# Moving two 8-byte state tiles behind the other pools of a fused scan and two-layer kernel

## The chip, the core and the metric

One core of a Trainium2 chip runs the whole program. The metric is the time of one execution in microseconds (us) as the device reports it; 2055.5 us is the median of three runs.

## The reference

For each of 4 sequences of 6080 steps with 256 features, a gated recurrence is computed, and its output goes through two matrix products with a squared ReLU between them:

```python
f = lower_bound + (1 - lower_bound) * sigmoid(f_logit)
for t in range(S):
    h = f[:, t] * h + (1 - f[:, t]) * x[:, t]
    y[:, t] = h
h = maximum(y.reshape(24320, 256) @ w_in, 0)     # w_in 256 x 2048
return h * h @ w_out                              # w_out 2048 x 256
```

Everything is float32. The kernel gets the precision on TensorE by splitting each operand into a high part (rounded to fp32r) and the rest (low part), and it takes three matmuls for one product: low weight with high data, high weight with high data, high weight with low data.

## The kernel before, in words

The 24,320 tokens lie along the free dimension, the 256 features on two blocks of 128 partitions. Tokens are taken in pairs of blocks of 512 (`pairs`, 23 pairs j = 0 to 22; the last pair, j = 23, has blocks of 384). For each pair, ScalarE, VectorE and GpSimd make the gate and the scan, and split the result into the tiles `xhi` and `xlo`, seven of each (`op_hi`, `op_lo`). Even pairs keep these in the pool `xA`, odd pairs in the pool `xB`.

The hidden layer has 16 blocks of 128 units, taken two at a time (q = 0 to 7). For the first two pairs (`plain`), each block is computed directly. From pair 2 on, `quad` computes two hidden blocks for two token blocks with seven products instead of eight (`product`, line 282, three matmuls each). The squared ReLU of the results is split again into `ghi` and `glo`, four pairs of tiles named `ghi00` to `ghi11` (`pair_of`, lines 316 and 317, in the pool `hid`). `layer2` (lines 303 to 305) multiplies them with the second layer's weights: six matmuls for each pair of tiles. In a quad the order on TensorE is written out: products P1, P5, P7; then `layer2` of the quad before for tile 00; P6, P2, P4, P3; then `layer2` for tiles 10, 01, 11. That is 21 matmuls with `xhi`/`xlo` as the moving operand ("x matmuls" below) and 24 with `ghi`/`glo` ("g matmuls"), 45 in a quad and 360 in a pair. Every matmul loads its own weights (PEld in the profile) while the matmul before it runs.

After a pair's last quad, `store` copies the sums on ScalarE into the one tile `osb` (line 312) and sends it out from SyncE's queue (line 313). It is called twice in the first quad of the next pair. The second call must wait until the first one's transfer has read the tile. In the quad behind it, ScalarE's copy at line 372 (`d`) is queued behind these copies, and P6 (the matmuls on `d`) needs it.

The order of instructions on each engine from the plain stage on is the program's own order (`manual_schedule`). The places of tiles in SBUF come from the pools: the pools of the left side follow each other in the order in which they are opened, and in a pool each tag follows the one before it, at the next multiple of 32 bytes. Starting bytes in a partition, as the program before has them:

| tiles | pool | start | start modulo 256 |
|---|---|---|---|
| weights `whi`, `wlo`, all 16, each column block of 128 | const | 16,608 and on, in steps of 512 | 224 |
| `xhi`, `xlo`, 14 tiles of 2048 bytes | xA | 106,720 and on | 224 |
| `f`, `x`, two buffers each of 4096 bytes | ld | 135,392 and on | 224 |
| `carry`, two buffers of 8 bytes | ld | 151,776 and 151,808 | 224, 0 |
| `ts` (sums for the products), two buffers | ld | 151,840 and on | 32 |
| `r`, `ghi`, `glo`, `s`, `c22`, `r22`, `c12` | hid | 155,936 and on (`ghi00` 160,032) | 32 |
| `osb`, 4096 bytes | outp | 188,704 to 192,800 | 32 |
| `xhi`, `xlo` of odd pairs (right side) | xB | 200,672 and on | 224 |

`carry` holds the last column of a pair's scan for the next pair; it is the only tile that isn't a multiple of 256 bytes long among the pools `xA`, `ld`, `hid` and `outp`.

Of the kernel before, what the change touches and what calls it, by code (L numbers as in the profile page):

```python
# [8 lines left out]
F32 = mybir.dt.float32  # L9
# [5 lines left out]
P = 128  # L15
# [17 lines left out]
def scan_then_relu2_kernel(  # L33
# [28 lines left out]
    KD = D // P  # L62
# [5 lines left out]
    ld = ctx.enter_context(tc.tile_pool(name="ld", bufs=1))  # L68
    hid = ctx.enter_context(tc.tile_pool(name="hid", bufs=1))
    outp = ctx.enter_context(tc.tile_pool(name="outp", bufs=1))  # L70
    ps = ctx.enter_context(tc.tile_pool(name="ps", bufs=1, space=bass.MemoryType.PSUM))

    xTv = xT.rearrange("(c p) t -> p c t", p=P)
# [16 lines left out]
    x_t, f_t, carry = {}, {}, {}  # L90
# [10 lines left out]
    def segments(t0, n):  # L101
        a = 0
        while a < n:
            s = (t0 + a) % seq
            m = min(n - a, seq - s)
            yield a, m, s == 0
            a += m
# [21 lines left out]
    def op_scan(j, t, c):  # L129
        t0, n = pairs[j]  # L130
        x = x_t[j, t]
        if t == 1 and c == 0:
            carry[j] = ld.tile([P, KD], F32, tag="carry", name=f"carry{j}", bufs=2)
        for a, m, new in segments(t0 + t * n, n):
            if new:
                init = 0.0
            elif a:
                init = x[:, c, a - 1 : a]
            elif t:
                init = x_t[j, 0][:, c, n - 1 : n]  # L140
            else:
                init = carry[j - 1][:, c : c + 1]
            nc.vector.tensor_tensor_scan(
                out=x[:, c, a : a + m], data0=f_t[j, t][:, c, a : a + m],
                data1=x[:, c, a : a + m], initial=init, op0=ALU.mult, op1=ALU.subtract,
            )
        if t == 1 and c == KD - 1 and j + 1 < NP:
            nc.vector.tensor_copy(carry[j][:, :], x[:, :, n - 1])
# [292 lines left out]
    def units(j):  # L441

        steps = []
        for t in range(2):
            for c in range(KD):
                steps.append([lambda t=t, c=c: op_sig(j, t, c), lambda t=t, c=c: op_f(j, t, c)])
                steps.append([lambda t=t, c=c: op_v(j, t, c)])
                steps.append([lambda t=t, c=c: op_scan(j, t, c)])

        def ready(*ks):  # L450
            out = []
            for k in ks:
                if k in MADE:
                    out.append(lambda k=k: op_sum(j, k, G))
                out += [lambda k=k: op_hi(j, k), lambda k=k: op_lo(j, k, G)]
            return out

        steps[6] += ready("B11")
        steps[7] += ready("B21")
        steps[9] += ready("T1")  # L460
        steps += [ready("T3"), ready("T2"), ready("T4"), ready("B22")]
        return steps

    def gate_ops(j, t, c, f_eng, lo_eng):
        k = f"B{c + 1}{t + 1}"
        return [
            lambda: op_sig(j, t, c),
            lambda: op_f(j, t, c, f_eng),
            lambda: op_v(j, t, c),
            lambda: op_scan(j, t, c),  # L470
            lambda: op_hi(j, k),
            lambda: op_lo(j, k, lo_eng),
        ]
# [52 lines left out]
    with tc.manual_schedule():  # L526
# [56 lines left out]
        j, q = before  # L583
# [45 lines left out]
```

## Time and profile before

| | |
|---|---|
| median of 3 runs | 2055.5 us (2054.15 to 2055.97) |
| the profiled execution's own time | 2055.8 us |
| its span, first to last instruction | 2054.0 us |
| TensorE (PE) busy, matmuls | 2002.1 us (97%), 8688 matmuls |
| weight loads (PEld) busy | 1627.1 us (79%) |
| VectorE (DVE) busy | 1536.5 us (75%) |
| ScalarE (ACT) busy | 1185.6 us (58%) |
| GpSimd (POOL) busy | 832.6 us (41%) |

A matmul's duration in the profile has a modelled end and overlaps with the next one's; the time from one matmul's start to the next one's start ("spacing" below) is what a matmul costs in an unbroken stream. Views of the trace print starts with two decimals of a microsecond, so a spacing over many matmuls is read from the first and the last start of the stretch.

### The profile page before, as it was taken

The page shows a single profiled execution, that of the slowest core. Times are in us where ns is not written, and L with a number is a line of the kernel's source. Part 1 is how long each engine was busy: PE and PEld are TensorE (multiplying, and loading weights), DVE is VectorE, ACT ScalarE, POOL GpSimd, SP SyncE. Part 2 cuts the span into 40 slices and gives each one's busy share as a digit, 9 for nine tenths or more (in the row PEclk, how much of TensorE's full clock was granted, in tenths as well). Part 3 has the DMA queues.
Part 4 walks back from the last instruction along what each step waited for, and adds up shares of the span by engine and source line. Part 5 has one row for each costly group of instructions (what it writes and reads, how often), then busy time and mean ns, then how long its engine had stood idle before and what let it go on. Part 6 is the DMA issues. An engine that isn't in the chain of part 4 may idle for free.

```text
span 2054.0 us, 24632 instructions
## 1 busy us (share of the span) xinstructions
PE 2002.1 (97%) x8688; PEld 1627.1 (79%) x8688; DVE 1536.5 (75%) x2283; ACT 1185.6 (58%) x2127; POOL 832.6 (41%) x712
## 2 busy tenths in 40 slices
PE   5999999999999999999999999999999999999998
PEld 3777787787878877878788787788887877878888
DVE  8975677777777777877778777777787777867765
ACT  4765555556555555555655555556555565555554
POOL 5747243443433424335344343443433424335332
PEclk9999999999999999999999999999999999999999
DMA  4211010101101011010110100101101011010000
GB/s 163 84 62 41 32 32 31 52 11 62 36 27 52 31 42 52 11 62 25 38 52 11 62 32 31 52 12 61 41 22 52 31 41 52 11 59 24 21 21 16
DMA packets 42013, 84.69 MB, mean 41 GB/s; under 512 B 2848, under 2 KB 4384, under 8 KB 41888
## 3 DMA queue, kind: packets, MB, share of 16 engines
q1 hardware_dynamic: 41888, 83.11, 12.1%
q8 instruction: 68, 1.11, 0.2%
q14 instruction: 57, 0.47, 0.1%
HBM read 58.20 MB, written 24.90 MB: 40 GB/s over the span
## 4 chain that ended last, share of the span: by engine, by line
PE 81%; DVE 6%; ACT 6%; DMA 4%; issue 2%; POOL 1%; SPq 0%; ACTq 0%; DVEq 0%; POOLq 0%
PE acc L303 14%; PE acc L305 14%; PE acc L304 14%; PE a L282 10%; PE c L282 10%; PE b L282 10%; PE d L282 6%; DMA out_dram<-osb 3%; ACT osb L312 2%; PE d L335 1%; DVE a L402 1%; DVE c L353 1%; ACT ghi L417 1%; DVE wy L223 1%; DVE c L392 1%
## 5 line engine op out<-in xcount | busy, mean ns | idle before, releaser
L303 PE MATMUL acc<-ghi,wlo 128*128 128x512 f32 (+1 forms) x1536 | 603.7, 393 | 6.1 <-ACT ghi L339 4.9
L305 PE MATMUL acc<-glo,whi 128*128 128x512 f32 (+1 forms) x1536 | 601.3, 391 | 3.3 <-DVE glo L343 3.1
L304 PE MATMUL acc<-ghi,whi 128*128 128x512 f32 (+1 forms) x1536 | 595.6, 388 | 0.0
L405 POOL TENSOR_TENSOR r<-r 128x512 f32<-128x512 f32 (+1 forms) x176 | 181.7, 1032 | 821.4 <-ACT ghi L403 622.7
L305 PEld LDWEIGHTS acc<-glo,whi 128*128 128x128 f32 x1536 | 288.8, 188 | 73.5 <-DVE glo L343 8.2
L303 PEld LDWEIGHTS acc<-ghi,wlo 128*128 128x128 f32 x1536 | 289.0, 188 | 66.0 <-ACT ghi L339 3.6
L304 PEld LDWEIGHTS acc<-ghi,whi 128*128 128x128 f32 x1536 | 288.9, 188 | 62.2
L356 ACT ACTIVATE ghi<-c 128x512 fp32r<-128x512 f32 (+1 forms) x176 | 110.6, 628 | 269.3 <-DVE c L353 269.3
L406 POOL TENSOR_TENSOR glo<-r,ghi 128x512 fp32r<-128x512 f32 (+1 forms) x176 | 226.7, 1288 | 13.8
L372 ACT ACTIVATE d<-a 128x512 f32<-128x512 f32 (+1 forms) x176 | 102.0, 579 | 210.1 <-PE a L282 209.6
L378 DVE TENSOR_TENSOR s<-b,s 128x512 f32<-128x512 f32 (+1 forms) x88 | 60.4, 686 | 215.4 <-ACT s L376 163.9
L182 POOL TENSOR_TENSOR xlo<-T,xhi 128x512 fp32r<-128x512 f32 (+1 forms) x88 | 114.2, 1297 | 137.8 <-ACT xhi L177 137.8
L358 DVE TENSOR_TENSOR glo<-c,ghi 128x512 fp32r<-128x512 f32 (+1 forms) x176 | 156.7, 890 | 2.8 <-ACT ghi L356 0.7
L378 DVE TENSOR_TENSOR s<-c,s 128x512 f32<-128x512 f32 (+1 forms) x88 | 60.3, 686 | 129.5 <-PE c L282 127.5
L182 POOL TENSOR_TENSOR xlo<-x,xhi 128x512 fp32r<-128x512 f32 (+1 forms) x72 | 93.0, 1293 | 146.5 <-ACT xhi L177 145.9
L282 PE MATMUL b<-xhi,wlo 128*128 128x512 f32 (+1 forms) x352 | 138.6, 394 | 0.3 <-DVE glo L419 0.3
L397 ACT ACTIVATE r<-a 128x512 f32<-128x512 f32 (+1 forms) x176 | 103.6, 589 | 61.1 <-PE a L282 61.1
L282 PE MATMUL a<-xhi,wlo 128*128 128x512 f32 (+1 forms) x352 | 138.8, 394 | 0.0
L282 PE MATMUL c<-xhi,wlo 128*128 128x512 f32 (+1 forms) x352 | 138.4, 393 | 0.0
L282 PE MATMUL a<-xlo,whi 128*128 128x512 f32 (+1 forms) x352 | 138.1, 392 | 0.0
L392 DVE TENSOR_TENSOR c<-d,s 128x512 f32<-128x512 f32 (+1 forms) x176 | 119.1, 677 | 24.8 <-PE d L282 20.5
L282 PE MATMUL b<-xlo,whi 128*128 128x512 f32 (+1 forms) x352 | 137.4, 390 | 0.0
(120 smaller groups left out, 4147.5 us busy)
## 6 DMA issues: line engine op xcount, KB each, us to landing
f<-in_fT_dram SPq DMA_DIRECT2D x46, 512.0 KB, 4.5
x<-in_xT_dram SPq DMA_DIRECT2D x46, 512.0 KB, 3.7
out_dram<-osb SPq DMA_DIRECT2D x46, 512.0 KB, 2.8
wraw<-in_wpack_dram SPq DMA_DIRECT2D x15, 512.0 KB, 3.3
f<-in_fT_dram SPq DMA_DIRECT2D x2, 384.0 KB, 3.5
x<-in_xT_dram SPq DMA_DIRECT2D x2, 384.0 KB, 3.2
out_dram<-osb SPq DMA_DIRECT2D x2, 384.0 KB, 2.4
wraw<-in_wpack_dram SPq DMA_DIRECT2D x2, 256.0 KB, 5.6
```

The source lines that it names most:

```text
L182: eng.tensor_tensor(out=xlo[j, i][:, :n], in0=block(j, k), in1=xhi[j, i][:, :n].bitcast(F32), op=ALU.subtract,)
L282: nc.tensor.matmul(bank[:, :n], lhsT=w, rhs=x[j, r][:, :n], start=start and m == 0, stop=m == 2, skip_group_check=True,)
L303: nc.tensor.matmul(acc, lhsT=lo, rhs=ghi[:, :n], start=first, stop=False)
L304: nc.tensor.matmul(acc, lhsT=hi, rhs=ghi[:, :n], start=False, stop=False)
L305: nc.tensor.matmul(acc, lhsT=hi, rhs=glo[:, :n], start=False, stop=last)
L356: nc.scalar.activation(out=ghi[:, :n], in_=c, func=AF.Copy)
L358: nc.vector.tensor_tensor(out=glo[:, :n], in0=c, in1=ghi[:, :n].bitcast(F32), op=ALU.subtract)
L378: nc.vector.tensor_tensor(out=sv, in0=bv, in1=sv, op=ALU.add)
L392: nc.vector.tensor_tensor(out=c22v, in0=dv, in1=sv, op=ALU.add)
L397: nc.scalar.activation(out=r11, in_=av, func=AF.Relu)
L405: nc.gpsimd.tensor_tensor(out=r22, in0=r22, in1=r22, op=ALU.mult)
L406: nc.gpsimd.tensor_tensor(out=lo22, in0=r22, in1=hi22.bitcast(F32), op=ALU.subtract)
```

## The change

A new pool `small` is opened after the pool `outp`, and the two buffers of `carry` are allocated there instead of in `ld`. Number of buffers, shapes, and all instructions with their order stay as they are.

```diff
     outp = ctx.enter_context(tc.tile_pool(name="outp", bufs=1))
+    small = ctx.enter_context(tc.tile_pool(name="small", bufs=1))
...
         if t == 1 and c == 0:
-            carry[j] = ld.tile([P, KD], F32, tag="carry", name=f"carry{j}", bufs=2)
+            carry[j] = small.tile([P, KD], F32, tag="carry", name=f"carry{j}", bufs=2)
```

The two places of 32 bytes go away from between `x` and `ts`. So `ts`, all of `hid` and `osb` start 64 bytes lower: `ts` at 151,776, `ghi00` at 159,968, `osb` at 188,640, and all of these starts are 224 modulo 256. The carried states lie at 192,736 and 192,768. Weights, `xA`, `f`, `x` and `xB` stay where they were.

## Rows read from the trace of the kernel before

**Rows 1.** The page: busy share of each engine, and granted clock in 40 slices.
```profile
PE 2002.1 (97%) x8688; PEld 1627.1 (79%) x8688; DVE 1536.5 (75%) x2283; ACT 1185.6 (58%) x2127; POOL 832.6 (41%) x712
...
PEclk9999999999999999999999999999999999999999
```

**Rows 2.** The page: the chain that ended last, share of the span by engine.
```profile
PE 81%; DVE 6%; ACT 6%; DMA 4%; issue 2%; POOL 1%; SPq 0%; ACTq 0%; DVEq 0%; POOLq 0%
```

**Rows 3.** Timeline of PE in pair 15 (start, duration): g matmuls, then nine x.
```profile
1327.14 0.39 PE L303 MATMUL acc<-ghi,wlo 128*128 128x512 f32 x1
...
1329.20 0.40 PE L282 MATMUL a<-xhi,wlo 128*128 128x512 f32 x1
...
1331.29 0.40 PE L303 MATMUL acc<-ghi,wlo 128*128 128x512 f32 x1
```

**Rows 4.** Timeline of PE in pair 16: eleven x spacings behind a stall, then g.
```profile
1406.01 0.50 PE L282 MATMUL d<-xhi,wlo 128*128 128x512 f32 x1 [0.61 <-ACT d L372]
1406.34 0.39 PE L282 MATMUL d<-xhi,whi 128*128 128x512 f32 x1
...
1408.84 0.40 PE L303 MATMUL acc<-ghi,wlo 128*128 128x512 f32 x1
...
1409.54 0.39 PE L303 MATMUL acc<-ghi,wlo 128*128 128x512 f32 x1
...
1410.23 0.39 PE L303 MATMUL acc<-ghi,wlo 128*128 128x512 f32 x1
```

**Rows 5.** Timeline of PE in pairs 4 and 5: the same stretch of eleven x spacings.
```profile
400.02 0.39 PE L282 MATMUL d<-xhi,whi 128*128 128x512 f32 x1
...
402.51 0.40 PE L303 MATMUL acc<-ghi,wlo 128*128 128x512 f32 x1
...
484.41 0.39 PE L282 MATMUL d<-xhi,whi 128*128 128x512 f32 x1
...
486.90 0.40 PE L303 MATMUL acc<-ghi,wlo 128*128 128x512 f32 x1
```

**Rows 6.** Timeline of PE: a pair's 360 matmuls between two stalls.
```profile
1322.20 0.50 PE L282 MATMUL d<-xhi,wlo 128*128 128x512 f32 x1 [0.60 <-ACT d L372]
1322.53 0.40 PE L282 MATMUL d<-xhi,whi 128*128 128x512 f32 x1
...
1325.06 0.40 PE L303 MATMUL acc<-ghi,wlo 128*128 128x512 f32 x1
...
1405.00 0.40 PE L305 MATMUL acc<-glo,whi 128*128 128x512 f32 x1
```

**Rows 7.** Windows of two pairs between stalls: us, busy (count) of each engine.
```profile
1322.20:1405.20 83.00, 83.00 (x360) 67.49 (x360) 63.57 (x93) 47.98 (x86) 32.90 (x27) 1.00 0.11 38
399.68:482.70 83.02, 83.02 (x360) 67.51 (x360) 63.66 (x95) 47.44 (x85) 32.90 (x27) 1.00 0.12 39
```

**Rows 8.** Timeline of ACT and PE before the stall of pair 15.
```profile
1313.83 0.40 PE L303 MATMUL acc<-ghi,wlo 128*128 128x512 f32 x1
...
1316.62 1.07 ACT L312 ACTIVATE osb<-acc 128x512 f32<-128x512 f32 x2
...
1320.57 1.09 ACT L312 ACTIVATE osb<-acc 128x512 f32<-128x512 f32 x2 [2.88 <-DMA out_dram<-osb]
...
1321.20 0.40 PE L305 MATMUL acc<-glo,whi 128*128 128x512 f32 x1
1321.54 0.60 ACT L372 ACTIVATE d<-a 128x512 f32<-128x512 f32 x1
```

**Rows 9.** Windows of the plain stage, in two parts.
```profile
41.00:135.00 94.00, 91.61 (x389) 72.03 (x388) 82.86 (x118) 62.85 (x111) 60.83 (x51) 1.00 0.26 88
135.00:190.00 55.00, 52.26 (x220) 40.38 (x219) 34.80 (x49) 29.48 (x52) 34.25 (x40) 1.00 0.11 34
```

**Rows 10.** Groups by line and form: ACT and POOL work on tiles of either start.
```profile
L406 POOL TENSOR_TENSOR glo<-r,ghi 128x512 fp32r<-128x512 f32 x168 | 218.6, 1301 | 13.2
...
L182 POOL TENSOR_TENSOR xlo<-T,xhi 128x512 fp32r<-128x512 f32 x84 | 110.1, 1310 | 131.1 <-ACT xhi L177 131.1
...
L401 ACT ACTIVATE ghi<-r 128x512 fp32r<-128x512 f32 x168 | 104.0, 619 | 0.0
...
L182 POOL TENSOR_TENSOR xlo<-x,xhi 128x512 fp32r<-128x512 f32 x69 | 89.9, 1305 | 140.7 <-ACT xhi L177 140.1
...
L177 ACT ACTIVATE xhi<-x 128x512 fp32r<-128x512 f32 x71 | 43.8, 617 | 9.4 <-DVE x L143 9.4
```

**Rows 11.** The chain in pair 15 (start, us): P6, P2, P4, P3, then g.
```profile
1332.82 0.70 PE d L282 x3
1333.52 0.69 PE a L282 x3
1334.21 0.70 PE b L282 x3
1334.91 0.68 PE c L282 x3
1335.59 0.23 PE acc L303
1335.83 0.24 PE acc L304
1336.07 0.23 PE acc L305
```

## The prediction, made before the changed kernel ran

> **What bounds the kernel now.** I read the page first. [...] What the page can't show is that the spacing isn't one number. For that I read the timeline of PE alone and divided stretches of starts by their count.
>
> In pair 15, nine g matmuls take 1329.20 - 1327.14 = 2.06 us, 228.9 ns each, and the nine x matmuls behind them 2.09 us, 232.2 ns each, with the same shapes and without a wait [rows 3]. In pair 16 eleven x spacings in a row take 2.50 us [rows 4], in pairs 4 and 5 the same stretch takes 2.49 us both times [rows 5]: 7.48 us over 33, so 226.7 ns each. I call this the floor. The same x matmuls thus run at 226.7 or at 232, and the reader is to see when. At the floor they follow a stall of PE; after it has been reached, it is held to the end of the x stretch, through four products, with other weights, other tiles and other PSUM banks. Then the first three g spacings take 1409.54 - 1408.84 = 0.70 us, 233 each, and the next three 0.69 us [rows 4]. So what ends the floor is the passage between x and g, and behind it each side needs some matmuls to settle: of four products in an unbroken stream, the last reaches the floor [rows 11].
>
> What differs between x and g is, as the layout of the program has it, the start of the moving tile: 224 modulo 256 for both x pools, as for all weights, and 32 for `ghi` and `glo`. That both parities of pairs reach the floor [rows 5] says that xA (224 modulo 512) and xB (480 modulo 512) are alike in this. My reading is that a passage between tiles of one class leaves the rhythm of the stream alone, and one between classes disturbs it.
>
> **The change part by part.** No instruction is added, removed or moved in any queue, SP's and POOL's among them, and no wait: the carry keeps two buffers. What changes is 64 bytes in the starts of `ts`, `hid` and `osb`, by which g gets the class of x and of the weights.
>
> *The steady part.* Pair 15 goes from its first matmul behind the stall, 1322.20, to its last one at 1405.00 [rows 6]. The first spacing there, 0.33, carries the end of the stall and stays. The other 358 take 1405.00 - 1322.53 = 82.47 us, 230.4 each. At the floor they take 358 x 0.2267 = 81.16 us. That is 1.31 us for a pair, and the window of pair 4 has the same length and count [rows 7], so I take it for all. Pairs 2 to 22 are 21 pairs: 27.5 us.
>
> *What comes back as a longer stall.* Each pair has one stall before P6: ScalarE copies into `osb` at 1316.62, waits 2.88 us for the transfer, copies again at 1320.57, and only then makes `d`, at 1321.54 [rows 8]. This chain starts from the pair's first quad and doesn't get faster. PE meanwhile runs 33 matmuls, from 1313.83 to 1321.20 plus one spacing, 7.60 us [rows 8]; at the floor 7.48. So PE arrives 0.12 us earlier at the same wait: 21 x 0.12 = 2.5 us are lost. A transfer from the moved `osb` could cost or give 0.1 us in each stall, 2 us in all; I take zero, since the size of its rows is the same.
>
> *Settling behind a stall.* Behind the stall of pair 15 the eleven spacings take from 1322.53 to 1325.06 [rows 6], 2.53 us against 2.49 at the floor; in pairs 4, 5 and 16 nothing is lost [rows 4, 5]. I take 0.03 for each pair, 0.6 us.
>
> *The plain stage.* There the g and x stretches have six matmuls each, so the passages are as frequent. But PE is idle for 94.00 - 91.61 = 2.4 us in the first part and 2.7 us in the second [rows 9], waiting for the engines that prepare weights and split the results. VectorE is at 82.86 of 94.00 us. If nothing is won there: 0. If all 609 matmuls won the 3.7 ns of the steady part: 2.2 us. I take 0.9, nearer to the lower end because the work of the other engines sets the pace.
>
> *Other engines.* ScalarE takes 619 ns for `ghi` from tiles of the old class and 617 for `xhi` from the class to come; GpSimd 1301 and 1305 [rows 10]. So the move is worth at most 4 ns in 1300 to them, either way, and their idle time covers it: at 81.7 us a pair VectorE would be busy for 63.6, 78% [rows 7]. If that cover failed, PE would wait and part of the gain would go: that is the upper half of the likeliest case's range.
>
> *The sum.* 27.5 - 2.5 - 0.6 + 0.9 = 25.3 us. The profiled execution took 2055.8 us, 1.8 more than its span; it lies 0.3 above the median. 2055.8 - 25.3 = 2030.5, and against the median 2030.2. I predict 2030 us.
>
> [...]
>
> **The rivals.** *Half of it:* the class that counts is modulo 512, not 256. Then x and g agree in even pairs (224 and 224) and not in odd ones (480 and 224). For it: no stretch shows a passage between 224 and 480, since g was at 288. Against it: x stretches of both parities settle to the same floor behind the same g [rows 5]. Pairs 2, 4, ... 22 are 11 of 21; 25.3 x 11/21 = 13.3 us, 2042.5 us.
>
> *No effect of the start:* the passage between x and g disturbs for another reason, such as the accumulation in long-lived banks that only `layer2` does, and stays as it is. For it: no stretch of the trace shows a passage between x and g of one class. Against it: inside the floor stretches the banks change every three matmuls and nothing happens [rows 4]. 2055.5 us.
>
> *Slower:* the class of x is itself the slow one, and g gets its 232.2 ns in place of 228.9 [rows 3]. All 358 spacings of a pair would then stand at 232.2 against 230.4: 0.64 us a pair, 13.5 us in all, 2069 us. It decides if the floor isn't a state to which the x stream comes by itself, but one that only a stall of PE sets; then the 21 stalls are too few to help. For it: the stretches of eleven at the floor stand behind a stall [rows 4, 5]. Against it: in an unbroken stream, with no stall ahead, the four products P6, P2, P4 and P3 take 0.70, 0.69, 0.70 and 0.68 us, so the fourth is at the floor (three times 226.7), and only the g behind it leave it again [rows 11]. But no x stretch is longer than twelve matmuls, so how the stream would go on isn't seen.
>
> *More comes back:* with PE 1.6% faster, waits that are now just covered appear in each quad. At 0.05 us for each of 168 quads this takes 8 us: 2038 us. VectorE's and ScalarE's shares [rows 7] speak against more than that; I count it to the likeliest case.
>
> **How the numbers follow.** The full effect: 0.75, 2030 us, its own range 2026 to 2038 (lower end: the plain stage's 1.3 us, no loss in stalls, 2.5, and no more). Half: 0.12, 2042.5. No effect: 0.07, 2055.5. Slower: 0.05, 2069. Something larger than the full effect: 0.01. The range that leaves out less than two in ten goes from 2026 to 2043. A measurement of this kernel can tell about 0.2% from no change, 4 us. Faster by more than that: 0.88; within it: 0.07; slower: 0.05.
>
> **What would show it.** If right, the timeline of PE in the middle of a pair shows x and g matmuls alike at 226 to 227 ns, and 45 matmuls of a quad take 10.20 us in place of 10.37; the mean durations of lines 303, 304 and 305, now apart, come together, as do those of line 282; the window between two stalls is 81.7 us for 360 matmuls; each stall before P6 is 0.1 us longer; all counts of instructions are the same. If odd and even pairs differ by 1.3 us, half of it was right. If spacings still change where x and g meet, the start isn't the cause, and the prediction is wrong from its first step. If the floor is there and PE's idle time has grown by more than 3 us, the step on stalls was mis-sized.

## The result and the profile after

The changed kernel took 2033.97 us in the median of 4 runs (2028.60 to 2035.81), the kernel before 2054.82 us. The ratio is 0.9894, with a 95% interval of 0.9873 to 0.9915. The profiled execution took 2035.8 us, with a span of 2034.0, where the one before had 2055.8 and 2054.0. The new line for the pool moves all line numbers behind it up by one: `layer2` is now 304 to 306, `product` 283.

The page's parts 1 and 4, to be held against [rows 1, 2]:

```profile
PE 1977.0 (97%) x8688; PEld 1628.5 (80%) x8688; DVE 1535.7 (75%) x2283; ACT 1186.1 (58%) x2127; POOL 828.7 (41%) x712
...
PE 80%; DVE 6%; ACT 6%; DMA 4%; issue 2%; POOL 1%; SPq 0%; ACTq 0%; DVEq 0%; POOLq 0%
```

The counts are the same and PE, busy for 97% of the span and with 80% of the chain, is still the bound; its busy time alone fell, by 25.1 us. VectorE, ScalarE and GpSimd are busy for what they were, within 4 us.

The timeline of PE in an undisturbed quad (start, duration), with a passage from g to x, from x to g, and both again; it answers to [rows 3] and [rows 11]:

```profile
1326.77 0.39 PE L283 MATMUL a<-xhi,wlo 128*128 128x512 f32 x1
...
1328.81 0.39 PE L304 MATMUL acc<-ghi,wlo 128*128 128x512 f32 x1
...
1330.17 0.39 PE L283 MATMUL d<-xhi,wlo 128*128 128x512 f32 x1
...
1332.89 0.39 PE L304 MATMUL acc<-ghi,wlo 128*128 128x512 f32 x1
```

Nine x matmuls take 2.04 us, six g 1.36, twelve x 2.72: 227 ns each, with no step where x and g meet. Before, nine x behind such a passage took 2.09. The groups by line show the same over the whole run (mean ns of one behind the bar):

```profile
L306 PE MATMUL acc<-glo,whi 128*128 128x512 f32 x1472 | 575.6, 391 | 3.7 <-DVE glo L344 3.0
L304 PE MATMUL acc<-ghi,wlo 128*128 128x512 f32 x1472 | 574.3, 390 | 6.8 <-ACT ghi L340 4.9 <-ACT osb L313 1.9
L305 PE MATMUL acc<-ghi,whi 128*128 128x512 f32 x1472 | 573.7, 390 | 0.0
L283 PE MATMUL a<-xhi,wlo 128*128 128x512 f32 x336 | 131.2, 390 | 0.0
```

All forms of 512 columns in the quads lie at 389 to 391, the first matmul on the bank `d` behind the stall aside (404). A modelled duration is about 163 ns more than the spacing (389.4 against 226.67 in the mean), so 389 to 390 is the floor. In the kernel before the same lines stood apart:

```profile
L303 PE MATMUL acc<-ghi,wlo 128*128 128x512 f32 x1472 | 582.3, 396 | 6.1 <-ACT ghi L339 4.9 <-ACT osb L312 1.3
L305 PE MATMUL acc<-glo,whi 128*128 128x512 f32 x1472 | 579.8, 394 | 3.3 <-DVE glo L343 3.1
L304 PE MATMUL acc<-ghi,whi 128*128 128x512 f32 x1472 | 574.1, 390 | 0.0
L282 PE MATMUL a<-xhi,wlo 128*128 128x512 f32 x336 | 133.4, 397 | 0.0
```

The stall of a pair, as in [rows 8] (engines together):

```profile
1301.15 0.63 ACT L401 ACTIVATE r<-c 128x512 f32<-128x512 f32 x1 [0.50 <-DVE c L393]
1301.21 0.39 PE L304 MATMUL acc<-ghi,wlo 128*128 128x512 f32 x1
...
1304.07 1.07 ACT L313 ACTIVATE osb<-acc 128x512 f32<-128x512 f32 x2
...
1308.01 1.08 ACT L313 ACTIVATE osb<-acc 128x512 f32<-128x512 f32 x2 [2.87 <-DMA out_dram<-osb]
...
1308.46 0.39 PE L306 MATMUL acc<-glo,whi 128*128 128x512 f32 x1
1308.98 0.60 ACT L373 ACTIVATE d<-a 128x512 f32<-128x512 f32 x1
1309.63 0.50 PE L283 MATMUL d<-xhi,wlo 128*128 128x512 f32 x1 [0.78 <-ACT d L373]
```

The last two lines of PE are 1.17 us apart where the pair's stall before had 1.00; less one spacing at the floor, a stall is 0.94 us here (0.96 in most pairs) and was 0.77 (0.78). "Stall" below is counted in this way; the idle time in brackets is shorter, since a matmul's modelled end reaches into it. The transfer holds ScalarE for 2.87 us as it did for 2.88. The list of waits has the idle time in total, first the kernel before and then the changed one (us in total, times, longest):

```profile
PE d L282 <- ACT d L372: 16.9, 22, 2.5
```

```profile
PE d L283 <- ACT d L373: 20.6, 22, 2.8
```

### The profile page after: what moved, and what is told of

It is laid out like the page before. It is cut to its first block, busy times and chain, and to the rows that moved or that the text cites. A ratio compares the mean times of both kernels' runs of the same rounds, so it can differ in the third digit from the quotient of the medians.

```text
span 2034.0 us, 24632 instructions
## 1 busy us (share of the span) xinstructions
PE 1977.0 (97%) x8688; PEld 1628.5 (80%) x8688; DVE 1535.7 (75%) x2283; ACT 1186.1 (58%) x2127; POOL 828.7 (41%) x712
## 4 chain that ended last, share of the span: by engine, by line
PE 80%; DVE 6%; ACT 6%; DMA 4%; issue 2%; POOL 1%; SPq 0%; ACTq 0%; DVEq 0%; POOLq 0%
PE acc L306 14%; PE acc L305 14%; PE acc L304 14%; PE a L283 10%; PE c L283 10%; PE b L283 10%; PE d L283 5%; DMA out_dram<-osb 4%; ACT osb L313 2%; DVE a L403 1%; DVE c L354 1%; ACT ghi L418 1%; DVE c L393 1%; ACT r L410 1%; ACT ghi L357 1%
## 5 line engine op out<-in xcount | busy, mean ns | idle before, releaser
L304 PE MATMUL acc<-ghi,wlo 128*128 128x512 f32 (+1 forms) x1536 | 595.6, 388 | 6.8 <-ACT ghi L340 4.9
L283 PE MATMUL a<-xhi,whi 128*128 128x512 f32 (+1 forms) x352 | 136.3, 387 | 0.0
L283 PE MATMUL c<-xlo,whi 128*128 128x512 f32 (+1 forms) x352 | 136.1, 387 | 0.0
L283 PE MATMUL c<-xhi,whi 128*128 128x512 f32 (+1 forms) x352 | 136.1, 387 | 0.0
```

The costliest lines, as they stand in the source:

```text
L283: nc.tensor.matmul(bank[:, :n], lhsT=w, rhs=x[j, r][:, :n], start=start and m == 0, stop=m == 2, skip_group_check=True,)
L304: nc.tensor.matmul(acc, lhsT=lo, rhs=ghi[:, :n], start=first, stop=False)
```

## The experiments

Each kernel was timed in turns with the kernel before on the same chip. "Settled pace" below is the mean of twelve spacings at the end of a quad's eighteen g matmuls, and "all" that of a quad's 45, each over the undisturbed quads of a trace (146 to 166 of 175, those in which no spacing reaches 0.3 us). The kernel before has 228.89 and 230.37 ns, the changed one 226.67 and 226.68.

**Is it the start of g?** The carry in its new place, `hid` put back:

```diff
+    gapp = ctx.enter_context(tc.tile_pool(name="gapp", bufs=1))
+    gap = gapp.tile([P, 16], F32, name="gap")
     hid = ctx.enter_context(tc.tile_pool(name="hid", bufs=1))
```

> The carry stays in its new pool, but 64 bytes left empty in front of the pool hid put g, r, s, c22, c12 and osb back to a start of 32 modulo 256; ts and the carry stay where the change put them. If the start of g sets the pace (theory), the spacings are those of before: g 228.9 ns, x 232 ns behind each passage, a pair 83.8 us, time 2054 to 2056. If the gain came from the place of the carry or of ts (rival), it stays at 2030 to 2036.

Measured (e1_hid_back): 2053.73 us, ratio to before 1.0000 (0.9991 to 1.0010); settled 228.89, all 230.37, the very spacings of before. So neither the carry's place nor that of `ts` did anything.

**Is it g alone?** `ghi` and `glo` in a pool of their own at 224, the rest of `hid` and `osb` at 32:

```diff
+    gp = ctx.enter_context(tc.tile_pool(name="gp", bufs=1))
+    gapp = ctx.enter_context(tc.tile_pool(name="gapp", bufs=1))
+    gap = gapp.tile([P, 16], F32, name="gap")
     hid = ctx.enter_context(tc.tile_pool(name="hid", bufs=1))
...
-        ghi = hid.tile(...)
-        glo = hid.tile(...)
+        ghi = gp.tile(...)
+        glo = gp.tile(...)
```

> Only ghi and glo start at 224 modulo 256; r, s, c22, r22, c12 and osb start at 32 as before the change, the carry is in its new pool. Theory (only what TensorE streams counts): all spacings at 226.7 ns, a pair 82.7 us, time 2030 to 2036 as with the whole change. Rival (the starts of what the other engines read and write, or of the stored tile, make part of it): above 2040, or a stall before P6 that differs from 0.95 us.

Measured (e2_g_alone): 2032.25 us, ratio 0.9894 (0.9880 to 0.9909); settled 226.67, all 226.68, stalls of 0.96 us. The start of the `ghi` and `glo` tiles is the whole of the gain, as far as these runs can tell; `r`, `s`, the sums and `osb`, which the other engines and the stores use, can lie at either start.

**Which modulus?** The first experiment with a gap of 128, 192, 32 and 224 bytes (`[P, 32]`, `[P, 48]`, `[P, 8]`, `[P, 56]`) in place of 64.

> 128 bytes left empty in front of hid: g starts at 96 modulo 256, which is 96 modulo 128 like x and the weights. If the class is the start modulo 128, all spacings are at 226.7 ns and the time is 2030 to 2036. If it is modulo 256, x and g disturb each other again and the time is about 2055.

Measured (e3_g_at_96): 2055.94 us, ratio 1.0011 (1.0001 to 1.0020); g settles at 233.33. The timeline of PE, g from its second triple:

```profile
1337.17 0.39 PE L306 MATMUL acc<-ghi,wlo 128*128 128x512 f32 x1
...
1340.66 0.39 PE L285 MATMUL a<-xhi,wlo 128*128 128x512 f32 x1
```

Fifteen in 3.49 us, 233 each. So 224 and 96, alike modulo 128, aren't alike for PE: modulo 128 is out. That the even and odd pairs of the changed kernel (xA at 224 and xB at 480 modulo 512, g and the weights at 224) run alike shows that modulo 512 isn't needed: two pairs in a row, from P6 behind one stall to about P6 behind the next (us, busy and count of PE, PEld, DVE, ACT, POOL, clock, DMA):

```profile
1309.63:1392.30 82.67, 81.90 (x360) 67.49 (x360) 63.55 (x93) 48.77 (x88) 32.78 (x27) 1.00 0.12 39
1392.30:1474.90 82.60, 81.89 (x360) 67.49 (x360) 63.61 (x95) 48.77 (x88) 32.78 (x27) 1.00 0.12 39
```

PE's busy time tells it, 81.90 and 81.89 us; the second window ends 0.1 us short of its P6.

> 192 bytes left empty in front of hid: g starts at 160 modulo 256, which is 32 modulo 128 (like before the change) and 32 modulo 64 (like x). If the class is modulo 128, the time is that of before, 2055, with the same spacings. If it is modulo 256 it lies off the floor too, but with other spacings; only if the class were modulo 64 would it be at 2030 to 2036, and then before the change it would have been so as well.

Measured (e4_g_at_160): 2058.80 us, ratio 1.0020 (1.0011 to 1.0029); settled 233.33, all 231.11. That rules out modulo 128 once more, and modulo 64 too; of the moduli tried, 256 is left. These two kernels are hardly slower than the one before although g runs at 233.33 in place of 228.89, because x gets back to the floor sooner: behind g at 96 after three spacings, at 160 after five, in the kernel before after ten.

> 32 bytes left empty in front of hid: g starts at 0 modulo 256, 32 above the weights and x, which stay at 224. By the distance, g has a steady pace of its own. If only whole steps of 64 count, it is that of 0 or of 64 (226.7 or 228.9 ns, 2034 or 2055); if each step of 32 counts, another one, and below 226.7 it would beat the changed kernel.

Measured (e10_g_at_0): 2060.54 us, ratio 1.0028 (1.0019 to 1.0037); settled 233.33, all 231.41.

> 224 bytes left empty in front of hid: g starts at 192 modulo 256, 32 below the weights and x. If only whole steps of 64 count, its pace is that of distance 0 or 192 (226.7 or 233.3 ns); if each step of 32 counts, another one. Time between 2030 and 2060.

Measured (e11_g_at_192): 2061.67 us, ratio 1.0036 (1.0024 to 1.0047); settled 233.33, all 231.41. No start of g that was tried beats 224. Steps of 32 count, as the run with g at 0 shows: it gives neither what 224 nor what 32 gave. Smaller steps weren't tried.

**Passage between moving tiles, or distance to the weights?** In all kernels so far x and the weights lay at 224. The next three take that apart, with 64 bytes ahead of the weights and 192 behind them; with 64 bytes behind the weights, and 192 at the right edge for xB; and with 64 ahead of the weights and 192 at the right edge:

```diff
# weights at 32
+    g0 = <64 bytes>
     cpool = ctx.enter_context(tc.tile_pool(name="const", bufs=1))
+    g1 = <192 bytes>
     xA = ctx.enter_context(tc.tile_pool(name="xA", bufs=1))
# x and g at 32
+    g1 = <64 bytes>
     xA = ctx.enter_context(tc.tile_pool(name="xA", bufs=1))
...
+    rgap = <192 bytes, side="right">
     prep_stack = ExitStack()
# all at 32
+    g0 = <64 bytes>
     cpool = ctx.enter_context(tc.tile_pool(name="const", bufs=1))
...
+    rgap = <192 bytes, side="right">
     prep_stack = ExitStack()
```

> The changed kernel with the weights alone moved: 64 bytes empty ahead of them and 192 behind, so that whi and wlo start at 32 modulo 256 and x and g, as in the changed kernel, at 224. If the distance between the moving tile and the weights that are loaded beside it sets the pace, every matmul runs as g did 192 above the weights (e4_g_at_160): 233 ns, a pair about 84.8 us, time about 2080. If only the passage between moving tiles of different starts disturbs (the prediction's reading), nothing changes: 226.7 ns, 2030 to 2036.

Measured (e5_w_at_32): 2073.65 us, ratio 1.0090 (1.0073 to 1.0107); settled 233.33, and all 233.33. Moving the weights alone, with x and g still at 224, makes every matmul slow. The groups by line:

```profile
L308 PE MATMUL acc<-ghi,wlo 128*128 128x512 f32 x1472 | 583.2, 396 | 5.6 <-ACT ghi L344 4.8 <-ACT osb L317 0.8
...
L287 PE MATMUL a<-xhi,wlo 128*128 128x512 f32 x336 | 132.9, 396 | 0.0
```

x and g have one pace, 396 in place of 390 of the changed kernel. The time is 6 us under the expected 2080: I had not taken off that each pair's stall gets shorter, 0.62 us against 0.96, when PE is slower; 21 x 0.34 is 7 us.

> x (both pools) and g all start at 32 modulo 256, the weights stay at 224: no passage between classes, but the moving tiles lie 64 above the weights. By the distance: every stretch settles to what g had before the change, 232, 226 and 229 ns, mean 228.9, a pair about 83.4 us, time about 2048. By the passage alone: 226.7 ns, 2030 to 2036.

Measured (e6_xg_at_32): 2043.31 us, ratio 0.9947 (0.9933 to 0.9962); settled 228.88, all 228.89. Nothing is left of a passage, not even the pattern of 232, 226 and 229 that was expected: each place in a quad has 228 to 229 ns. But the pace isn't the floor. A pair takes 83.37 us, as expected; the time is 5 us under the expected 2048, 2 us of it because the stalls are shorter (0.85). The same groups:

```profile
L306 PE MATMUL acc<-ghi,wlo 128*128 128x512 f32 x1472 | 577.6, 392 | 5.5 <-ACT ghi L342 3.9 <-ACT osb L315 1.6
...
L285 PE MATMUL a<-xhi,wlo 128*128 128x512 f32 x336 | 131.7, 392 | 0.0
```

> Weights, x (both pools) and g all start at 32 modulo 256. By the distance (0 as in the changed kernel): 226.7 ns everywhere, 2030 to 2036. If 32 is a slow start in itself, whatever the weights have: 228.9 ns, about 2048.

Measured (e7_all_at_32): 2032.12 us, ratio 0.9887 (0.9873 to 0.9902); settled 226.67, all 226.67. The start itself doesn't count; the distance does. All weights of a kernel lie at one start modulo 256, so the runs don't tell whether the distance to a matmul's own weights counts or that to the weights that are loaded while it runs. Settled paces by the distance from the weights' start up to that of the moving tile, modulo 256:

| distance | 0 | 32 | 64 | 128 | 192 | 224 |
|---|---|---|---|---|---|---|
| ns for a 512-column matmul | 226.67 | 233.33 | 228.89 | 233.33 | 233.33 | 233.33 |

**Where did part of the gain go?** The second store of a pair is issued one quad later, behind the copies `d` and `s`, so that `d` isn't queued behind a wait for the first store's transfer. Once on the changed kernel and once on the kernel before:

```diff
+    late_store = []
...
         next(left, None)
+        for s_late in late_store:
+            store(*s_late)
+        late_store.clear()
         slots(0)
...
             if pq == NQ - 1:
-                store(pj, 1)
+                late_store.append((pj, 1))
```

> The changed kernel, with the second store of a pair (copies into osb and the transfer) issued one quad later, behind ScalarE's copies d and s and the start of tail12, so that d no longer waits for the transfer of the first store. If the stall before P6 gave back part of the gain: the 21 stalls of 0.96 us and the 0.11 us behind each go, about 22 us less than the changed kernel, 2009 to 2014, with 81.6 us a pair. If another wait stands right behind it, a pair stays above 82.2 us and the time above 2022.

Measured (e8_late_store): 2006.83 us (2006.17 to 2007.71), ratio to before 0.9766 (0.9752 to 0.9781): the fastest kernel of this study. The wait on `d`, 22 times and 20.6 us in the changed kernel, is there once, behind the plain stage, and ScalarE makes `d` and `s` before it copies into `osb`:

```profile
PE d L283 <- ACT d L374: 1.9, 1, 1.9
```

```profile
1290.68 0.58 ACT L374 ACTIVATE d<-a 128x512 f32<-128x512 f32 x1 [1.04 <-PE a L283]
1291.36 0.60 ACT L378 ACTIVATE s<-c 128x512 f32<-128x512 f32 x1
...
1293.97 1.07 ACT L313 ACTIVATE osb<-acc 128x512 f32<-128x512 f32 x2
```

A pair takes 81.60 us, 360 x 226.67: PE never stops (busy for 1569.00 of the 1569.00 us from 391 to 1960 us). It is 27.1 us under the changed kernel, more than the 22 expected, and so under the expected range. The profiled executions differ by 28.1: 24.8 in the pairs, where the long stall late in the run is gone too, with the lowered clock behind it (below; 1.00 is granted in that window), and 3.1 ahead of them, where traces scatter by as much (also below).

> The kernel before, with the same later store as in e8_late_store. If the stall before P6 takes back part of what faster matmuls win, the change is worth more without the stall: this kernel loses 21 stalls of 0.78 and the 0.11 behind each, 18.7 us (2035 to 2038), and lies 28 us above e8_late_store, where the change itself moved 22 us. If the stall has nothing to do with it, the distance to e8_late_store is about 22 us.

Measured (e9_late_store_before): 2035.20 us, ratio 0.9903 (0.9888 to 0.9917). Without the stall the move of g is worth 2035.20 - 2006.83 = 28.4 us (29 when each is taken from the kernel before on its own chip), with it 20.9, in an interval of 17 to 26. In the pairs, which is the firmer measure: from 82.93 to 81.60 us, 1.33, without the stall; from 83.81 to 82.71, 1.10, with it. So the stall gave back a sixth of each pair's gain, 0.23 us or 5 us in all; the rest of the 7 us between the two differences is of the size of the lowered clock's 1.4 us and the scatter of 1.8 us below.

## Why the prediction was right

The cause, the start of g's tiles, and roughly the amount held: 25.3 us were forecast, the medians differ by 20.9, and the profiled executions by 20.0. How the start acts was only half understood.

*The steady part* was sized right. The 27.5 us forecast, less 0.6 for settling, are 26.4 in the trace: behind the stall a pair had 1.31 us above the floor, and has 0.04 (the last of the 21 stretches, which runs into the shorter blocks, gave 1.0). The floor read from eleven spacings [rows 4, 5] is the pace of the whole kernel.

*The longer stall* was mis-sized: 0.18 us for each of the regular ones (0.78 to 0.96) and not 0.12. I had let ScalarE's chain begin with the first g matmul behind P3. The rows show where it does: `r22` (line 400 before, 401 after) waits for VectorE's sum, and that for P6. In the kernel before it stands 0.12 us ahead of the first g matmul, after the change 0.06:

```profile
1313.71 0.63 ACT L400 ACTIVATE r<-c 128x512 f32<-128x512 f32 x1 [0.46 <-DVE c L392]
...
1313.83 0.40 PE L303 MATMUL acc<-ghi,wlo 128*128 128x512 f32 x1
```

From `r22` to `d` the chain took 7.83 us in both traces. PE runs ahead of it from P6 on, so what it wins in P6, P2, P4 and P3, another 0.05 us, comes back as well. All stalls of pairs 2 to 22 took 3.5 us more, where 2.5 were forecast. The prediction had named a growth of over 3 us as the sign that this step was mis-sized.

*What the sum didn't have:* the one long stall late in the run grew to 2.76 us of idle time, and behind it the granted clock fell: five spacings of 0.42 to 0.43 us in place of 0.23, and a granted clock of 0.72 over the window 1805 to 1811 us (the column behind POOL), of 0.50 from 1807.3 to 1810.7.

```profile
1807.78 0.79 PE L283 MATMUL d<-xhi,wlo 128*128 128x512 f32 x1 [2.76 <-ACT d L373]
1808.37 0.63 PE L283 MATMUL d<-xhi,whi 128*128 128x512 f32 x1
1808.79 0.63 PE L283 MATMUL d<-xlo,whi 128*128 128x512 f32 x1
```

```profile
1805.00:1811.00 6.00, 3.24 (x9) 2.61 (x9) 2.73 (x4) 2.98 (x6) 0.00 (x0) 0.72 0.24 88
```

It cost 1.4 us. The trace of before had a granted clock of 1.00 there (window 1822 to 1832 us), behind 2.48 us of idle time. That the longer stall brought the clock down isn't shown: in the trace of e2_g_alone the granted clock was 1.00 at the same place, behind 2.87 us.

```profile
1808.16 0.50 PE L286 MATMUL d<-xhi,wlo 128*128 128x512 f32 x1 [2.87 <-ACT d L376]
```

```profile
1805.00:1811.00 6.00, 3.13 (x14) 2.36 (x13) 2.34 (x3) 3.11 (x6) 0.00 (x0) 1.00 0.22 87
```

*The plain stage* gave nothing, where 0.9 us were taken between 0 and 2.2. The first copy `d`, which ends it, starts at 219.3 us in the trace of before and 221.1 after:

```profile
L373 ACT ACTIVATE d<-a x176: 475/582/605, 221.1 to 2017.2; 128x512 f32<-128x512 f32 x168, 128x384 f32<-128x384 f32 x8
```

The other traces say that this 1.8 us is scatter: 217.4, 218.6, 219.0 and 218.6 with g off the floor (the first, third and fourth experiment and the late store on the kernel before), 216.6, 218.8 and 217.9 with g on it. The means are 218.6 both times, with before and after counted in. PE waits there for other engines, as [rows 9] had it; in the changed kernel's trace the longest such wait between 41 and 190 us, 1.9 us, is for ScalarE's copy into `osb`. The 221.1 is the latest of all the traces; the others lie between 216.6 and 219.4. In the profiled run of the changed kernel a stall of 1.9 us from 131 us on was followed by a lower granted clock as well, 0.50 from 134.8 to 138.1 us and about 1.6 us in spacings, which the trace of before doesn't have there (1.00): the window 131 to 141 us has 0.83:

```profile
131.00:141.00 10.00, 8.08 (x29) 6.16 (x28) 4.66 (x7) 5.60 (x10) 3.95 (x6) 0.83 0.17 65
```

In sum 26.4 - 3.5 - 1.4 - 1.8 = 19.7 of the 20.0 us in the profiled executions.

*The explanation* of the pace, though, was half right. I had put all of it on the passage between moving tiles of different starts. The passage exists: behind it x needs some ten matmuls to come back to its pace [rows 11]. But with x and g at 32 there is no passage and 228.89 ns, and with the weights alone at 32 there is none either and 233.33. The distance between the moving tile and the weights sets the pace, and the passage is the way from one pace to the other. In the kernel before, g had its own 228.89, and x, at distance 0, had the floor as its pace but was seldom given the time to reach it. The prediction came out right because the change put both at distance 0, where the passage goes away and the pace is the floor; that both readings give the same here is luck, and on e5_w_at_32 and e6_xg_at_32 the prediction's own would have failed. The rival of an effect modulo 512 fell with the equal pairs, the one of a slow x class with the changed kernel's own x matmuls at 226.67, the one without an effect of the start with e1_hid_back and e2_g_alone, and the one of waits that appear in each quad with e8_late_store, where PE runs a pair without any.

Why the distance acts isn't shown by any run here; only the paces are: with the weights alone moved by 64 bytes a matmul went from 226.67 to 233.33 ns.

## What to carry to other kernels

Where PE streams without a break and its spacing changes between stretches of equal shape, compare the starts of the moving tiles and of the weights modulo 256, the one left of the moduli tried here: a small tile between two pools can move them, as two of 8 bytes did here by 64 bytes, with 228.89 ns for g in place of 226.67. Read the pace from starts over a counted stretch, not from the share of busy time, which was 97% in both kernels. And before a gain on the bound engine is booked, look for the wait that it will reach earlier: here the wait for a store's transfer kept 5 us of this gain, and one moved store removed the whole wait, 19 us of the kernel before and 27 of the changed one.

## What the runs showed that was not expected

The paces are exact: 226.67, 228.89 or 233.33 ns, the same to 0.02 in the mean over the undisturbed quads of kernels of different layout. Only distances 0 and 64 of the six tried are better than 233.33. A matmul whose spacings alternate (237 and 229 ns at distance 128) has the same settled mean as one with equal spacings (233 at 192). Likewise at distance 64: the 232, 226 and 229 of g before and the even 229 of e6_xg_at_32 have one mean, 228.89.
